# A hand-ordered queue by due time for the second network's first gemm, with copied seeds and swapped banks

## The chip, the cores and the metric

The kernel runs on one core of a Trainium2 chip. TensorE (PE in the profile) does the matmuls, VectorE (DVE), ScalarE (ACT) and GpSimd (POOL) the elementwise work, and SyncE (SP) issues nearly all DMAs. The metric is the device time of one execution in microseconds; the figure for the kernel is the median of its timed runs.

## The reference

Attention in chunks of 64 rows, then two feed-forward networks, each with a wide hidden layer, all in fp32:

```python
x = attn_out.transpose(0, 2, 1, 3).reshape(4608, 512)
h = x @ w1_in                     # 512 -> 2048
x = leaky_relu(h, 0.01) @ w1_out  # 2048 -> 512
h = x @ w2_in                     # 512 -> 2048
P = a[0] + a[1]*h + a[2]*h*h + a[3]*h*h*h
Q = 1 + abs(b[0])*abs(h) + abs(b[1])*h*h
out = (P / (Q + 1e-6)) @ w2_out   # 2048 -> 512
```

## The kernel before

The 4608 rows are cut into nine blocks of 512 columns (the data lie transposed). PE works in a format that keeps only part of an fp32 mantissa, so every operand is split into a high part (an ACT copy into that format) and a low part (a DVE subtract), and each product is three matmul passes: high by high, high by low, low by high (`PASSES`, L417). One matmul is 128x128 by 128x512.

The first part (start-up and the loop at L1134) runs attention and the first network block by block: `gemm1` (L550) is 12 matmuls, `gemm2` (L582) 12 matmuls, two of the eight PSUM banks (`hh_ps`) hold the first gemm's results in turn, four (`o_acc`) the second's. Beside it the second network's weights are decoded and staged to DRAM (`stage_w`, L414). The finished blocks go to DRAM as `xd`, through four `ypool` buffers. One step of 24 matmuls makes one of 16 hidden slices `f` of a block.

`second` (L733) does the rest. Its first loop (L889) makes block 8's first network, its second (L927) block 0's second network. Between the two parts `hh_ps` grows from two banks to four (L1181).

Then come 32 *units* (L1019), eight for each of four pairs of blocks. A unit makes two hidden slices of both blocks of the pair by a Strassen-like form: seven `product`s (L972, 6 matmuls each) take the place of eight, of ready-made sums of the weights (`wa`, S1 to S4) and of the blocks (`T1` to `T4`, made by POOL in `sums_make`, L748), and of plain parts (A11, A12, A22 with `B11`, `B21`, `B22`). The results lie in four banks a, b, c, d. In the order of the queue: `a = A11·B11`, ACT copies a to SBUF (L1043), `b = A12·B21`, DVE adds the copy onto b (L1048); `a += S2·T2`, ACT copies a (L1055); `a += S3·T3`, ACT copies a (L1062); `c = S1·T1`, DVE forms `d = c + copy` (L1067); `a += A22·T4`; `c += S4·B22`, and DVE adds the second copy onto c (L1091). Between the products stand three or four *tasks* (`task`, L825): the 12 matmuls of the second gemm for one earlier hidden slice.

The rational function of a bank pair is ten kinds of steps. `begin` (L982) runs on ACT: two times `Abs` (L992), the linear part of Q over both (L993), two times the linear part of P (L863). `act_q` (L866) is on POOL; `act_p1`, `act_p2` (L869, L872) on DVE read the bank; `act_l` is a reciprocal root and a square on ACT (L875, L876); `act_r`, `act_g` (L879, L882, L883) are three 128x1024 DVE instructions. `pre`/`split` (L821, L808) then make the high part (ACT, L813) and the low part (DVE, L814) for the next task just ahead of it. At a change of pair the new blocks' forms are loaded (`x_load`) and split (`x_split`, L769: a 128x1024 ACT copy and a 128x1024 DVE subtract), and where a block's 16 tasks end, `finish` (L617) empties the four `o_acc` banks. After the units 20 tasks remain.

Every engine works off its own queue in the order of the program text (`manual_schedule`): there is no planner in this part, the order is that of the lines L1019 to L1115.

Of the kernel before, what the change touches and what calls it, by code (L numbers as in the profile page):

```python
# [9 lines left out]
F32 = mybir.dt.float32  # L10
# [33 lines left out]
NPAIRS = 4  # L44

# [169 lines left out]
def tile_kernel(ctx: ExitStack, tc: tile.TileContext, qt, kt, vt, w1, w2, a, b, out):  # L215
# [40 lines left out]
    xf = [dram.tile([4, P, 2, TM], F32, name=f"xf{j}") for j in range(NPAIRS)]  # L256

# [312 lines left out]
    def act1b(i, f):  # L570
        t = gt[0, i, f]
        gh, gl = (gpool.tile([P, TM], F32R, tag=g, name=f"{g}0_{i}_{f}")[:, :BLOCKS[i]] for g in ("gh", "gl"))
        nc.scalar.activation(out=gh, in_=t, func=AF.Copy)  # L573
        gt[0, i, f] = gh, gl, t
# [42 lines left out]
    def finish(ph, i, share=False, cut=False):  # L617
        n = BLOCKS[i]
        for dc in range(KC):
            y = ypool.tile([P, TM], F32, tag="y", name=f"y{ph}_{i}_{dc}")[:, :n]  # L620
            dst = out[dc, :, starts[i]:starts[i] + n] if ph else xd[i][dc]
            for c, r in enumerate([slice(0, n // 2), slice(n // 2, n)] if cut and dc == KC - 1 else [slice(0, n)]):
# [4 lines left out]
                nc.sync.dma_start(out=dst[:, r], in_=y[:, r])  # L627

# [99 lines left out]
    FORMS = ("B11", "B21", "T2", "T3", "T1", "T4", "B22")  # L728
# [4 lines left out]
    def second(npool):  # L733
# [14 lines left out]
        def sums_make(j, q, t, eng):  # L748
            kc, c = q // 2, slice(q % 2 * 256, q % 2 * 256 + 256)
            for x, a, b, op in ((3, 3, 1, "subtract"), (1, 1, 0, "subtract"), (0, 3, 0, "add"), (2, 2, 0, "subtract")):  # L750
                eng.tensor_tensor(out=t[:, x], in0=t[:, a], in1=t[:, b], op=getattr(ALU, op))
            for x, nm in ((1, "T1"), (0, "T2"), (3, "T3"), (2, "T4")):
                nc.sync.dma_start(out=xf[j][SUMS[nm]][:, kc, c], in_=t[:, x])
# [3 lines left out]
        def x_load(j, n):  # L757
# [3 lines left out]
            i0, i1 = blocks_of(j)  # L761
            if nm in SUMS:
                src = xf[j][SUMS[nm]]
            else:
                i, k = {"B11": (i0, 0), "B21": (i0, 2), "B22": (i1, 2)}[nm]
                src = xd[i][k:k + 2].rearrange("k p n -> p k n")
            nc.sync.dma_start(out=t[:, 1].bitcast(F32), in_=src)

        def x_split(j, n):  # L769
            t = xform[j, FORMS[n]]  # L770
            S.activation(out=t[:, 0], in_=t[:, 1].bitcast(F32), func=AF.Copy)
            V.tensor_tensor(out=t[:, 1], in0=t[:, 1].bitcast(F32), in1=t[:, 0].bitcast(F32), op=ALU.subtract)
# [18 lines left out]
        def load_o(q):  # L791
            t = wo[q] = wpool.tile([P, 2, 2, DM], F32R, tag=TAGO[q % 3], name=f"wo{q}")
            for x in range(2):
                nc.sync.dma_start(out=t[:, x].bitcast(F32), in_=wd[2 * (q % HALF) + x][:, :, 1, :])

# [6 lines left out]
        for j in range(NPAIRS):  # L802
            for i in blocks_of(j):
                tasks.extend((1, i, f) for f in range(NF))
        halved, done = [0], [0]
        free, left_of = [], {}
# [426 lines left out]
```

## Time and profile before

| | us |
|---|---|
| median of the timed runs (lowest, highest) | 1741.75 (1740.11, 1743.24) |
| the profiled execution | 1752.58 |
| its span, first to last instruction | 1750.7 |
| mean granted share of the TensorE clock | 0.975 |

The profile is one execution. Busy time of an engine is the time in which one of its instructions ran; matmuls overlap in the pipeline, so a matmul's listed duration is longer than its share of PE's time. The clock of PE is listed as a share of the full one (2.4 GHz); 0.5 is the lower of its two levels (1.2 GHz).

### The profile page before, as it was taken

To read this page: it belongs to the slowest core of one execution; us is meant where nothing else is said; L and a number is where in the kernel's file an instruction comes from. 1 tells how busy PE (TensorE), PEld (TensorE's weight loads), DVE (VectorE), ACT (ScalarE), POOL (GpSimd) and SP (SyncE) were. 2 spreads that over 40 slices of the span, in tenths; PEclk is the share of its full clock that TensorE was granted. 3 is DMA by queue.
4 is the path that set the end of the run, shared out by engine and by line. 5 is a ranking of instruction groups with operands and counts; after the bars stand their busy time and mean duration, and the time that the engine had idled before them with its cause. 6 is when DMAs were issued, how large, how long until landed. Compare 5 with 4: busy or idle time off the path is not lost.

```text
span 1750.7 us, 24111 instructions
## 1 busy us (share of the span) xinstructions
PE 1653.1 (94%) x9198; PEld 1340.8 (77%) x9198; DVE 1210.7 (69%) x1825; ACT 926.6 (53%) x1418; POOL 260.4 (15%) x157
## 2 busy tenths in 40 slices
PE   8999999999999999999999988899989998899989
PEld 7888788888888888888777776677767776677767
DVE  8984766565656665632875787877878787877772
ACT  7653233333333333334766676666667666666652
POOL 0000000000000000000222341243213332122110
PEclk9999999999999999999999998999989999999999
DMA  7631324343343343326645675567556675556425
GB/s 273 221 109 43 101 92 139 103 133 119 111 144 115 119 129 124 100 94 207 210 139 177 203 260 181 183 211 238 204 175 223 216 262 192 167 179 196 141 89 182
DMA packets 143571, 284.71 MB, mean 163 GB/s; under 512 B 12384, under 2 KB 45408, under 8 KB 138208
## 3 DMA queue, kind: packets, MB, share of 16 engines
q1 hardware_dynamic: 143024, 282.51, 48.5%
q8 instruction: 73, 1.20, 0.3%
q10 hardware_dynamic: 432, 0.66, 0.1%
q14 instruction: 42, 0.34, 0.1%
HBM read 229.64 MB, written 53.48 MB: 162 GB/s over the span
## 4 chain that ended last, share of the span: by engine, by line
PE 67%; ACT 18%; DVE 10%; issue 3%; DMA 1%; POOL 0%; SPq 0%; ACTq 0%; DVEq 0%; POOLq 0%
PE hh L558 23%; PE hh L975 11%; PE oa L591 10%; PE ob L591 10%; PE oa L836 5%; PE ob L836 4%; ACT u L993 3%; DVE gl L814 3%; ACT ah L992 3%; ACT l L876 2%; ACT sa L863 2%; ACT l L875 2%; ACT gh L813 2%; ACT sb L863 1%; PE at L458 1%
## 5 line engine op out<-in xcount | busy, mean ns | idle before, releaser
L558 PE MATMUL hh<-x,w 128*128 128x512 f32 x1920 | 459.9, 390 | 0.1
L558 PEld LDWEIGHTS hh<-x,w 128*128 128x128 f32 x1920 | 359.7, 188 | 75.4 <-DVE x L543 0.5
L866 POOL TENSOR_TENSOR u<-u,ah 128x1024 f32<-128x1024 f32 x64 | 163.8, 2559 | 559.2 <-ACT u L993 556.4
L567 ACT ACTIVATE t<-hh 128x512 f32<-128x512 f32 x128 | 76.5, 597 | 315.2 <-PE hh L558 301.5
L836 PE MATMUL oa<-gh,wo 128*128 128x512 f32 x576 | 215.6, 414 | 15.1 <-DVE y L624 7.6
L975 PE MATMUL hh<-xf_T,wa 128*128 128x512 f32 x576 | 162.9, 432 | 62.5 <-ACT s L1043 62.4
L836 PE MATMUL ob<-gh,wo 128*128 128x512 f32 x576 | 202.2, 392 | 0.0
L975 PEld LDWEIGHTS hh<-xf_T,wa 128*128 128x128 f32 x576 | 115.3, 205 | 99.1 <-ACT s L1043 75.6
L578 DVE TENSOR_TENSOR gl<-t,gh 128x512 fp32r<-128x512 f32 x128 | 88.3, 690 | 144.0 <-ACT gh L573 140.0
L591 PE MATMUL oa<-gh,w 128*128 128x512 f32 x512 | 182.0, 396 | 0.0
L591 PE MATMUL ob<-gh,w 128*128 128x512 f32 x512 | 178.4, 389 | 0.0
L836 PEld LDWEIGHTS oa<-gh,wo 128*128 128x128 f32 x576 | 117.6, 204 | 44.9 <-DVE y L624 10.2
L992 ACT ACTIVATE ah<-hh 128x512 f32<-128x512 f32 x128 | 69.5, 596 | 126.7 <-DVE hh L1091 86.5
L486 POOL TENSOR_TENSOR e<-e,sm 128x512 f32<-128x512 f32 x23 | 24.0, 1044 | 710.4 <-DVE sm L482 710.4
L836 PEld LDWEIGHTS ob<-gh,wo 128*128 128x128 f32 x576 | 109.6, 190 | 23.7
L836 PE MATMUL oa<-gl,wo 128*128 128x512 f32 x288 | 120.0, 417 | 6.4 <-DVE gl L814 6.4
L836 PE MATMUL ob<-gl,wo 128*128 128x512 f32 x288 | 112.6, 391 | 0.0
L591 PEld LDWEIGHTS oa<-gh,w 128*128 128x128 f32 x512 | 96.1, 188 | 21.2
L591 PEld LDWEIGHTS ob<-gh,w 128*128 128x128 f32 x512 | 96.1, 188 | 20.2
L591 PE MATMUL oa<-gl,w 128*128 128x512 f32 x256 | 99.9, 390 | 0.0
L494 DVE STREAM_TRANSPOSE pt<-e 32x256 f32<-32x256 f32 x224 | 97.5, 435 | 3.2
L591 PE MATMUL ob<-gl,w 128*128 128x512 f32 x256 | 99.6, 389 | 0.0
(172 smaller groups left out, 2794.3 us busy)
## 6 DMA issues: line engine op xcount, KB each, us to landing
wo<-wd SPq DMA_DIRECT2D x144, 512.0 KB, 5.3
wa<-ws SPq DMA_DIRECT2D x32, 1024.0 KB, 5.1
raw<-in_w SPq DMA_DIRECT2D x46, 512.0 KB, 4.8
wb<-wd SPq DMA_DIRECT2D x32, 512.0 KB, 4.3
q<-in_q SPq DMA_DIRECT2D x36, 256.0 KB, 3.6
raw<-in_w SPq DMA_DIRECT2D x9, 1024.0 KB, 5.0
v<-in_v SPq DMA_DIRECT2D x36, 256.0 KB, 4.1
k<-in_k SPq DMA_DIRECT2D x34, 256.0 KB, 4.0
```

Of the source, the lines that this page charges most:

```text
L494: nc.vector.transpose(pt[c + b:c + b + 32, :, a:a + 32], e[c + a:c + a + 32, :, b:b + 32])
L558: nc.tensor.matmul(ps, w[wp][:, 0, kc * P:(kc + 1) * P], x[:, xp, kc, :], start=(kc == 0 and (wp, xp) == (0, 0)), stop=(kc == KC - 1 and ( ...
L567: nc.scalar.activation(out=t, in_=ps, func=AF.Prelu, alpha=0.01)
L578: nc.vector.tensor_tensor(out=gl, in0=t, in1=gh.bitcast(F32), op=ALU.subtract)
L591: nc.tensor.matmul(o_acc(dc, n), w[wp][:, 1, dc * P:(dc + 1) * P], g[gp], start=(first and (wp, gp) == (0, 0)), stop=(last and (wp, gp) == ...
L814: V.tensor_tensor(out=gl, in0=g, in1=gh.bitcast(F32), op=ALU.subtract)
L836: nc.tensor.matmul(o_acc(dc, TM), w[:, wp, c] if ph else wt[0, f][wp][:, 1, c], g[gp], start=(f == 0 and (wp, gp) == (0, 0)), stop=(f == N ...
L863: S.activation(out=t, in_=h, func=AF.Identity, scale=nega[:, 3:4], bias=nega[:, 2:3])
L866: G.tensor_tensor(out=u, in0=u, in1=ah, op=ALU.mult)
L975: nc.tensor.matmul(bank, wform[:, wp, kc * P:kc * P + P], x[:, xp, kc, :], start=start and kc == 0 and (wp, xp) == PASSES[0], stop=stop an ...
L992: S.activation(out=ah[:, x], in_=h[x], func=AF.Abs)
L993: S.activation(out=uu, in_=ah, func=AF.Identity, scale=absb[:, 1:2], bias=absb[:, 0:1])
```

## The change

What it does, in the order of the program:

- While blocks 2 to 7 run, finished blocks are read back from `xd`, split on ACT and DVE, and their high and low parts are stored in a new DRAM array `xs` (18 pieces of 128x512; six more are done in the units). The forms B11, B21, B22 are then loaded split, 1 MB each instead of 512 KB, and need no `x_split`.
- `hh_ps` stays at two banks (d and c in the units); the other two become one tile `hab` of two banks, a and b. From unit to unit a and b change places.
- In a unit the copies go into banks as starting values: ACT copies a into b (PE then accumulates A12·B21 onto it) and a into c (PE accumulates S1·T1 and S4·B22). S3·T3 goes into d alone, is copied to SBUF by ACT, and DVE adds it onto a and forms `d = c + copy`. So DVE has two adds instead of three.
- The steps on the pair (a, b) read both banks with one 128x1024 instruction; those on (c, d) stay 128x512.
- High and low parts are made for two hidden slices at a time (`split_hi`, `split_lo`, 128x1024), further ahead of the task than before.
- Each step of the units and of the tasks behind them is put in a list with a due time (`at`), unit `u` at `20.43*u` plus an offset; the list is sorted and issued in that order.
- Five units have three tasks (before: four units), so 21 tasks remain after the units instead of 20. Block 8's second gemm accumulates in the banks of a to d, and the last two tasks of block 7 stand behind the first four of block 8.

```diff
+UNIT = 20.43
+            if ph == 0 and 0 < i < NB - 2 and (i % 2 or dc > 1):
+                later.append((i, dc))
+    def split_out(i, dc, y):
+        half = xs[(i - 1) // 2][dc // 2 if i % 2 else 2]
+        hi, lo = (ypool.tile([P, TM], F32R, tag="y", name=f"y{c}{i}_{dc}") for c in "hl")
+        nc.scalar.activation(out=hi, in_=y, func=AF.Copy)
+        nc.vector.tensor_tensor(out=lo, in0=y, in1=hi.bitcast(F32), op=ALU.subtract)
+        for c, z in enumerate((hi, lo)):
+            nc.sync.dma_start(out=half[:, c, dc % 2, :], in_=z.bitcast(F32))
+    def reload(i, dc):
+        y = ypool.tile([P, TM], F32, tag="y", name=f"yr{i}_{dc}")
+        nc.sync.dma_start(out=y, in_=xd[i][dc])
+        return y
...
+        FEWER = {0: 0, 1: 1, 2: 3, 4: 1, 5: 3}
+        SLOTS = (1.36, 5.45, 13.62, 17.7)
+        order = [(u, x) for u in range(NU2) for x in range(4) if x != FEWER.get(u)] + [(NU2, x) for x in range(NF + 8)]
...
+        def split_hi(p):
+            t0, t1 = tasks[2 * p:2 * p + 2]
+            g, sub, first = twos.pop(t0)
...
+            S.activation(out=gh, in_=g, func=AF.Copy)
+        def split_lo(p):
...
+            gl = gpool.tile([P, 2, TM], F32R, tag="g", name=f"gl_{p}")
+            V.tensor_tensor(out=gl, in0=g, in1=gh.bitcast(F32), op=ALU.subtract)
...
+        for p in range(HALF + 1, len(tasks) // 2):
+            u, x = when[2 * p]
+            if u < NU2:
+                hi, lo = ((-UNIT + 8.35, -UNIT + 14.3), (-UNIT + 10.2, 1.4), (-UNIT + 10.2, 1.4), (8.35, 14.3))[x]
...
         for u in range(NU2):
             j, k = divmod(u, HALF)
+            a, b = ab[:, u % 2], ab[:, 1 - u % 2]
+            mm(0.0, "A11", "B11", a, True)
+            mm(4.09, "S2", "T2", a, False)
+            mm(1.36 if FEWER.get(u) == 0 else 8.17, "S3", "T3", d, True)
+            mm(9.53, "A22", "T4", a, False)
+            mm(10.9, "A12", "B21", b, False)
+            mm(12.26, "S1", "T1", c, False)
+            mm(16.34, "S4", "B22", c, False)
...
+            at(u, 1.45, copy, b, a)
+            at(u, 5.5, copy, c, a)
+            at(u, 9.6, keep)
+            at(u, 12.3, add, a, a)
+            at(u, 13.6, add, d, c)
+            at(u, 13.0, lin, u, 0)
+            at(u, 14.2, mag, u, 0)
+            at(u, 15.2, lin, u, 1, 1)
+            at(u, 16.0, den, u, 0)
+            at(u, 17.2, mag, u, 1, 1)
+            at(u, 17.9, lin, u, 1, 0)
+            at(u, 18.7, mag, u, 1, 0)
+            at(u, 19.3, den, u, 1)
+            at(u, UNIT + 2.2, root, u, 0)
+            at(u, UNIT + 3.5, square, u, 0)
+            at(u, UNIT + 6.1, root, u, 1)
+            at(u, UNIT + 7.2, square, u, 1)
+            at(u, 17.4, den_q, u, 0)
+            at(u, 20.6, den_q, u, 1)
+            at(u, 15.6, cube, u, 0, 0)
+            at(u, 16.8, cube, u, 0, 1)
+            at(u, 18.1, cube, u, 1, 0, 1)
+            at(u, 18.8, cube, u, 1, 1, 1)
+            at(u, 19.5, cube, u, 1, 0, 0)
+            at(u, 20.2, cube, u, 1, 1, 0)
+            at(u, UNIT + 4.4, rest, u, 0)
+            at(u, UNIT + 8.4, rest, u, 1)
...
+                        at(u, 12.35 + 1.05 * x, sums, k - 2, x)
...
+                    at(u, 2.65, x_lo, j + 1, 1)
+                    for x, t in enumerate((1.42, 5.48, 9.58, 10.95, 12.28)):
+                        at(u, t, x_load, j + 1, 2 + x)
+                    at(u, 11.3, x_hi, j + 1, 2)
+                    at(u, 12.4, x_hi, j + 1, 3)
+                    at(u, 12.35, x_lo, j + 1, 2, G)
+                    at(u, 14.0, x_lo, j + 1, 3, G)
+                    at(u, UNIT + 0.7, x_hi, j + 1, 5)
+                    at(u, UNIT + 2.65, x_lo, j + 1, 5)
+        for _, _, fn, args in sorted(events):
+            fn(*args)
...
+                split_later()
                 if f != 1:
                     stage_w()
                 if f in (3, 6, 9, 11, 13):
                     stage_w()
+                if f > 1:
+                    reload_later()
...
-        hh_ps.extend(singles(ps_open("hhq", "right"), "hh2", "hh3"))
+        at_new = ps_open("hhq", "right").tile([P, 2, TM], F32, name="hab")
```

In the new names `lin`, `mag`, `den`, `den_q`, `root`, `square`, `cube` and `rest` are the steps L863, L992, L993, L866, L875, L876, L869 with L872, and L879 with L882 and L883; `add` is a DVE add, `keep` and `copy` are ACT copies, `mm` is a `product`. `G` is POOL.

## Rows read from the trace of the kernel before

**Rows 1.** The page's first parts: span, and the granted clock by slices.

```profile
span 1750.7 us, 24111 instructions
...

```

**Rows 2.** The cores' view: span and mean granted clock.

```profile
core 0: 1750.7 us, clock 0.975
```

**Rows 3.** Stretches: length, busy PE, PEld, DVE, ACT, POOL (instructions), clock, DMA share, GB/s.

```profile
40.00:826.00 786.00, 785.98 (x5221) 645.42 (x5220) 489.71 (x938) 304.31 (x514) 25.31 (x24) 1.00 0.37 122
...
910.00:1747.00 837.00, 749.73 (x3074) 599.85 (x3072) 623.31 (x735) 533.01 (x737) 216.17 (x113) 0.95 0.58 193
...
913.00:1684.00 771.00, 692.69 (x2836) 554.74 (x2837) 595.40 (x699) 508.46 (x701) 212.54 (x111) 0.95 0.59 197
```

**Rows 4.** PE's waits, 910 us to the end: us in total, times, longest.

```profile
PE hh L975 <- ACT s L1043: 62.4, 27, 4.2
PE oa L836 <- DVE y L624: 7.6, 6, 1.7
PE oa L836 <- DVE gl L814: 6.4, 8, 1.3
PE oa L836 <- ACT gh L813: 4.2, 1, 4.2
PE oa L836 <- ACT y L626: 3.2, 1, 3.2
PE hh L975 <- DVE sa L872: 2.7, 1, 2.7
```

**Rows 5.** The chain that ended last, through one unit: start, us, what.

```profile
1393.74 0.62 DVE hh L1091
...
1394.44 1.09 ACT ah L992 x2
...
1400.79 0.49 ACT s L1043
...
1401.32 1.66 PE hh L975 x6
```

**Rows 6.** PE's timeline later in that unit: start, us, line, count.

```profile
1405.54 2.88 PE L975 MATMUL hh<-xf_T,wa 128*128 128x512 f32 x12
1408.26 1.52 PE L975 MATMUL hh<-xf_T,wb 128*128 128x512 f32 x6
```

**Rows 7.** Stretches, PE alone, behind waits of 1.71 and 2.97 us.

```profile
1417.00:1424.00 7.00, 5.29 (x24) 1.00 0.98 362
...
1444.00:1452.00 8.00, 5.03 (x17) 0.80 0.07 26
```

**Rows 8.** Single lines on DVE and POOL: ns least/median/most, first and last start.

```profile
L879 DVE SCALAR_TENSOR_TENSOR u<-u,l x64: 1215/1218/1768, 943.0 to 1696.0; 128x1024 f32<-128x1024 f32 x64
...
L772 DVE TENSOR_TENSOR xf_B<-xf_B x12: 1215/1218/1219, 839.9 to 1511.9; 128x1024 fp32r<-128x1024 f32 x12
...
L1048 DVE TENSOR_TENSOR hh<-hh,s x32: 683/691/700, 920.6 to 1667.7; 128x512 f32<-128x512 f32 x32
...
L866 POOL TENSOR_TENSOR u<-u,ah x64: 2359/2405/3414, 931.1 to 1686.3; 128x1024 f32<-128x1024 f32 x64
```

**Rows 9.** The timeline where POOL and DVE overlap: start, us, engine, line.

```profile
1119.57 2.79 POOL L866 TENSOR_TENSOR u<-u,ah 128x1024 f32<-128x1024 f32 x1 [15.53 <-ACT u L993]
1120.03 2.87 DVE L814 TENSOR_TENSOR gl<-sa,gh 128x512 fp32r<-128x512 f32 x1
```

**Rows 10.** Groups in the units: shapes, count, busy us, mean ns, idle before.

```profile
L993 ACT ACTIVATE u<-ah,absb 128x1024 f32<-128x1024 f32 x63 | 78.4, 1244 | 2.1
L875 ACT ACTIVATE l<-u,cst 128x1024 f32<-128x1024 f32 x62 | 70.8, 1142 | 0.0
...
L1043 ACT ACTIVATE s<-hh 128x512 f32<-128x512 f32 x32 | 18.5, 578 | 2.5 <-PE hh L975 2.5
...
L883 DVE SCALAR_TENSOR_TENSOR gn<-gn,nega,u 128x1024 f32<-128x1024 f32 x17 | 21.8, 1285 | 0.6
```

More of the change, by code (lines that the diff above doesn't have):

```diff
@@ L731, in tile_kernel, with second @@
     NU2 = NPAIRS * HALF
-    def second(npool):
+    def second(npool, at_new):
         S, G = nc.scalar, nc.gpsimd
@@ L898, in second @@
             if 4 <= f < 8:
-                sums_make(0, f - 4, st[f - 4], V)
+                for x in range(4):
+                    sums_make(0, f - 4, st[f - 4], V, x)
             if 2 <= f < 6:
@@ L970, in second, with product @@
         live = {}
-        def product(wform, x, bank, start, stop):
+        ab, (d, c) = at_new, hh_ps[:2]
+        def product(wform, x, bank, start):
             for kc in range(2):
@@ new lines, in den_q, with root, square, cube @@
+        def den_q(u, r):
+            act_q(*live[u, r][1:3])
+        def root(u, r):
+            v = live[u, r]
+            S.activation(out=v[1], in_=v[2], func=AF.Abs_reciprocal_sqrt, bias=cst[:, 0:1])
+        def square(u, r):
+            v = live[u, r]
+            S.activation(out=v[1], in_=v[1], func=AF.Square)
+        def cube(u, r, step, x=None):
+            t = live[u, r][0]
+            (act_p1, act_p2)[step](ab if x is None else (c, d)[x], t if x is None else t[:, x])
+        def rest(u, r):
+            v = live.pop((u, r))
+            act_r(v[2], v[1])
+            act_g(v[2], v[1], v[0])
@@ new lines, in second @@
+        for n in range(2 * HALF, len(tasks)):
+            ph, i, f = tasks[n]
+            if f == NF - 1 and n + 1 < len(tasks):
+                u, x = when[n]
+                t = SLOTS[x] if u < NU2 else 2.72 * x
+                for dc in range(KC):
+                    eng = (S, V, S, V)[dc] if x < 3 or u == NU2 else (V, V, S, S)[dc]
+                    at(u, t + 0.72 + (0.64 if u == NU2 or x < 3 else 0.9) * dc, put, i, dc, eng)
+        at(0, 1.5, finish_one, NF - 1)
+        back = {}
@@ new lines, in add @@
+            def add(to, of, u=u):
+                V.tensor_tensor(out=to, in0=of, in1=live[u, 2], op=ALU.add)
+            if u == 0:
+                at(u, 0.05, lambda b=b: nc.tensor.matmul(b, wb[0][:, 0, 0:P], xform[0, "B11"][:, 0, 0, :], start=True, stop=True))
+            at(u, 1.45, copy, b, a)
[5 more added lines that the diff above has]
+            at(u, 14.2, mag, u, 0)
```

308 lines of the change are left out of this document (152 added, 156 removed).

## Prediction, made before the changed kernel ran

> **What bounds the kernel now.** I read the page first, then the stretches, then PE's waits, then the chain through one unit.
>
> The page gives a span of 1750.7 us and shows the granted clock below full only in the last part [rows 1]. The stretches say the same: from 40 to 826 us PE is busy for 785.98 of 786.00 us at full clock, so nothing but fewer matmuls could shorten that part, and ACT and DVE have room there (304 and 490 us of 786). From 910 to 1747 us PE is busy for 749.7 of 837 us, with 3072 matmuls (1344 in products, 1728 in tasks; the row counts two more at its edges), at a clock of 0.95 [rows 3].
>
> The pace of matmuls without waits: twelve start within 1408.26 - 1405.54 = 2.72 us, 0.2267 us each [rows 6]. So 3072 matmuls need 696.4 us, and the 837 us hold some 140 us of something else. Two things make it up.
>
> Waits: 62.4 us in 27 of the 32 units for the copy L1043, and 24.1 us in 17 others, 86.5 us in all [rows 4]. A listed matmul lasts 2.88 - 11 x 0.2267 = 0.39 us [rows 6], and the next one may start after 0.23, so each vanished wait also gives back 0.16 us of pipeline end: 44 x 0.16 = 7.0 us.
>
> Clock: the mean over the run is 0.975 [rows 2], and it is 1.00 before 910 us, so 0.025 x 1750.7 = 43.8 us of full-rate time are lost behind 910 us. Part of that falls into waits; with PE busy for 749.7 of 837 us [rows 3], 0.896 x 43.8 = 39.2 us hit matmuls. The fall to the lower level (1.2 GHz) comes behind the longer waits: clock 0.80 around a wait of 2.97 us, 1.00 around one of 1.71 us [rows 7].
>
> 86.5 + 7.0 + 39.2 = 132.7 us; the remaining 8 us are short hand-overs.
>
> Why the copy is late: S2·T2 accumulates on a, so it needs L1043's copy of a. That copy is behind, on ACT, all of the previous unit's (c, d) work, which starts only when DVE has finished the add L1091: from 1393.74 (add) through ACT's queue to 1400.79 (copy) and PE at 1401.32 [rows 5]. It is a ring through DVE, ACT and PE, and PE has only 24 matmuls (5.44 us) to cover a chain of 7.6 us.
>
> **The change part by part.**
>
> *The ring is cut.* In the new queue, L1091's add is gone (c is seeded before its products), and ACT comes to the seed copy with nothing left behind: its last step of the unit before, `den` at 19.3, lasts 1.24 us [rows 10] and ends at 20.5, and A11·B11 ends at 20.43 + 1.36 + 0.16 = 21.95. I lay out one unit, times from its start. A seed copy into PSUM by ACT is not in this trace; an ACT copy out of PSUM takes 0.58 [rows 10], a DVE instruction that writes PSUM 0.69 to 0.70 [rows 8]. I take 0.58, the same engine. It ends at 2.1 (2.2 with the dearer price); S2·T2 is due at 4.09: 1.9 us to spare. Then root and square (at most 1.14 each [rows 10]) to 4.4, the second seed 5.6 to 6.2 for S1·T1 at 12.26. The other links: `add` on a needs A22·T4 (10.9) and `keep`, the add into d needs S1·T1, so 13.8 to 14.5, and S4·B22 on c, due at 16.34, has 1.8 us to spare. DVE's `split_lo` follows, 1.22 [rows 8], to 15.7, for the task at 17.7: 2 us to spare. Then two `cube` steps on (a, b); a 128x1024 instruction from PSUM is not shown; between 1.22 to 1.29 (128x1024 from SBUF [rows 8, 10]) and 1.40 (twice the 0.70 of a 128x512 one with a PSUM operand [rows 8]) I take 1.29, as the fixed part is paid once. They end at 18.3 and free the bank of the next A11·B11 at 20.43: 2.1 us to spare, 1.9 by the dearer price. No product stands behind a chain without at least 1.8 us of cover.
>
> *Load of the engines.* ACT: 508.5 us in 32 units = 15.9 each [rows 3]; nothing but the two PSUM destinations gets dearer, up to 2 x 0.12, and of seven `x_split` copies per pair four stay: under 16.2 of 20.43. DVE: 595.4 / 32 = 18.6 [rows 3]; one add less (0.69), and five of seven `x_split` subtracts per pair less (two stay on DVE, two go to POOL, three end): 5 x 1.22 / 8 = 0.76. So 17.15. Against this stands the lock between POOL and DVE. A DVE instruction with both sources in SBUF that starts while POOL runs lasts until POOL is done and then its own time: 2.87 us in place of 0.69 beside a POOL instruction [rows 9]; one with a PSUM operand keeps its 0.69 to 0.70 throughout [rows 8]. The new `split_lo` due at 1.4 meets `den_q` of the unit before (due 0.17, 2.4 us [rows 8], to 2.6): 1.2 us of waiting. The one due at 14.3 meets pieces of `sums` in half the units, up to 1.05 by their due times: 0.5 on average. 17.15 + 1.2 + 0.5 = 18.9 us of 20.43, 1.5 to spare. The first wait ends the subtract at 3.8, before the task at 5.45 and `rest` at 4.4.
>
> *The other waits.* L624 and L626 (10.8 us): where a block's tasks end, the next task used to stand right behind; now at least a product or more lies between (next slot 4.09 us later, four copies at about 0.6 on two engines). L814 and L813 (10.6): high and low parts are made at least 1.6 us ahead, as laid out. L872 (2.7): unit 0 begins with products in banks of its own; but its S3·T3 uses d, one of the only two banks that the loop of block 0 now has, so I leave 1.2 us there. At the three changes of pair two subtracts stand on POOL in front of `den_q` and may hold DVE's `split_lo` past 17.7: 0.5 us each. Behind unit 31 `rest` and a `split_lo` share DVE ahead of the fourth task: 1.3 us. Left over: 4 us.
>
> *What is added elsewhere.* 18 pieces in blocks 3 to 7: an ACT copy (0.58), a DVE subtract (0.69) and three 256 KB DMAs each, in steps of 5.44 us, 24 matmuls. ACT would rise from 39% to 40% and DVE from 62% to 64% there [rows 3]; a step's first-gemm bank is needed again only two steps later, which hides a few us of delay. I cost it at nothing; with that cover gone it would be 18 x 1.3 = 23 us. The DMA share of the units, 0.59 over 771 us [rows 3], becomes about 0.59 x 24.1 / 20.43 = 0.70. On SP the loads of the next pair's forms stand behind a weight load that waits for its task: the one due at 1.42 leaves at 4.1, and its copy is due at 11.3. With two banks in place of four, block 8's loop still gives ACT 2.72 us from the end of one gemm to the next use of its bank. Nothing here.
>
> **The sum**, on the profiled execution: 1750.7 - 132.7 + 4 = 1622.0 span, with 1.9 us around it 1623.9. The median is 1741.75 against 1752.58 for that execution, 0.9938 of it: 1614 us. The floor is 910 + 696.4 + 4 (behind the last matmul) = 1610 span, 1602 in the median's terms.
>
> **The rivals.**
>
> *The clock goes on falling* although the long waits go. For it: PE would still have short hand-overs. Against it: the row of a 1.71 us wait at full clock [rows 7]. It gives back 39 us: 1653. On this the Trainium skill, "TensorE: Matmul & The Clock Gate", section "A second HAM failure mode: psum-queue depth-cycling", tells of a kernel in which short but frequent idling between groups of matmuls made the clock swing between its levels. By that rule this rival; by the trace, the forecast.
>
> *DVE becomes the bound.* 18.9 of 20.43 leaves 1.5. If one `den_q` falls into `rest`, whose sources are all in SBUF, DVE needs 18.9 + 2.4 = 21.3, and each unit 0.9 us more: 32 x 0.9 = 29, so 1643.
>
> *The wait only changes its place*, so the change does not do what it says: another link (a seed, the add into d) holds PE about as long per unit, 62 us of wait and the clock with it. Only the 24 us of other waits go: about 1717. Against it: every link has 1.8 us to spare in the layout.
>
> *Slower.* The queues are fixed by due times. If ACT's `den` on (c, d) comes 1.8 us late, its `den_q` ends at 4.4 instead of 2.6 and runs into `rest`; DVE falls behind, everything slides, and both `den_q` and all `sums` end up against instructions with SBUF sources. DVE then needs 18.9 + 4.8 + 1.6 = 25.3 us a unit, 4.9 over PE's: 32 x 4.9 = 157, so 1771. It decides against the change from 4.0 us a unit on (128 us in all). For it: the lock is in the rows [rows 9]. Against it: `den` would have to be late on an engine with 4 us of room per unit.
>
> **How the numbers follow.** Forecast 0.60 (own range 1602 to 1632), DVE bound 0.15 (to 1658), clock 0.12 (1653), wait elsewhere 0.07, slower 0.06. The likeliest is the forecast, 1614. The range from the floor, 1602, to 1658 holds the first three, 0.87; a narrower one would cut into the clock's case. Faster by over 0.2% (about what a measurement of this kernel can tell) are all but the last: 0.93; 0.01 for the same; 0.06 slower.
>
> **What would show it.** Right: a stretch from 910 us to the end about 133 us shorter, PE's waits under 10 us in total, clock 1.00 behind 910 us, 20.4 us a unit. DVE bound: PE waits for DVE lines, DVE busy over 95% in the units, low parts of 3 us and more. The clock: waits gone, mean clock still 0.975. Wrong altogether: units of 24 us, or PE idle between 215 and 826 us, where the 18 pieces run.

## The result, and the profile after

The changed kernel takes 1623.76 us (median of four executions, 1622.95 to 1624.04). The kernel before takes 1742.49 beside it (median of four, 1740.11 to 1753.17). The ratio is 0.9307 with an interval of 0.9268 to 0.9345: 6.9% faster, 119 us less. The forecast was 1614 in a range of 1602 to 1658. The span came out at 1620.7 where the sum said 1622.0.

The page of the kernel after: span, busy times with their share and count, PE's busy tenths in 40 slices, and the granted clock in the same slices.

```profile
span 1620.7 us, 24054 instructions
...
PE 1603.5 (99%) x9199; PEld 1317.1 (81%) x9199; DVE 1211.5 (75%) x1665; ACT 908.8 (56%) x1292; POOL 264.3 (16%) x163
...
PE   8999999999999999999999999999999999999998
...
PEclk9999999999999999999999999999999999999999
```

PE is busy from end to end, and the clock never shows a fall. Before, two slices of the same line are below nine tenths, both in the last part, and the mean was 0.975 [rows 2]:

```profile
PEclk9999999999999999999999998999989999999999
```

Stretches of the kernel after, columns as in [rows 3]: the first part, all behind 910 us, the units, and three units in which POOL makes no sums.

```profile
40.00:826.00 786.00, 784.87 (x5215) 644.59 (x5215) 504.30 (x954) 313.43 (x531) 25.97 (x24) 1.00 0.43 140
...
910.00:1617.00 707.00, 701.32 (x3082) 577.00 (x3080) 612.78 (x561) 508.06 (x596) 218.53 (x119) 1.00 0.71 242
913.00:1567.00 654.00, 649.05 (x2854) 534.36 (x2852) 594.87 (x545) 497.39 (x583) 217.79 (x119) 1.00 0.73 248
1434.84:1496.04 61.20, 61.20 (x272) 50.68 (x270) 54.72 (x49) 44.44 (x52) 14.42 (x6) 1.00 0.58 194
```

The stretch behind 910 us was 837 us with 749.73 of them busy on PE [rows 3]. It is 707 us now, with about as many matmuls. 3082 of them at 0.2267 us each [rows 6] need 698.7, so 8.3 us are left of the 140 that were lost. The last row is three units in which PE is busy for all of 61.20 us: 20.40 a unit, 90 matmuls at that pace. The first part is as long as it was, with DVE and ACT a little fuller.

PE's waits from 910 us to the end: us in total, times, longest, as in [rows 4].

```profile
PE hh L903 <- DVE gl L887: 1.3, 1, 1.3
PE hab L1063 <- DVE gn L953: 1.2, 1, 1.2
PE hab L1063 <- DVE sb L953: 1.1, 1, 1.1
PE hab L903 <- ACT yl L935: 0.7, 1, 0.7
PE hab L1063 <- ACT hab L1176: 0.7, 1, 0.7
PE oa L903 <- DVE gl L887: 0.6, 1, 0.6
```

Six waits of 5.6 us in place of 44 of 86.5 us. None repeats from unit to unit.

The start of one unit at 1312.44, where the two events lie that the layout was worked out for: the seed copy and the lock between POOL and DVE. Columns: start, us, engine, line, operation, count, idle time before and its releaser.

```profile
1312.44 1.52 PE L1063 MATMUL hab<-xf_B,wb 128*128 128x512 f32 x6
...
1312.54 2.39 POOL L947 TENSOR_TENSOR u<-u,ah 128x1024 f32<-128x1024 f32 x1 [0.85 <-ACT u L1102]
1312.79 3.23 DVE L887 TENSOR_TENSOR gl<-sb,gh 128x1024 fp32r<-128x1024 f32 x1
...
1314.00 0.58 ACT L1176 ACTIVATE hab<-hab 128x512 f32<-128x512 f32 x1 [1.53 <-PE hab L1063]
...
1316.52 0.84 PE L1063 MATMUL hab<-xf_T,wa 128*128 128x512 f32 x3
```

The counts of the last row end with the view, at 1317. ACT stood idle for 1.53 us, waiting for the product A11·B11, so in this unit nothing was queued ahead of the copy any more. The copy ends at 1314.58, and S2·T2, which may write a from then on, starts at 1316.52: 1.94 us of cover where [rows 5] had a wait. The low part (L887) started under `den_q` (POOL L947) and ended 3.58 us into the unit.

Single lines of the kernel after: ns least/median/most, first and last start.

```profile
L1176 ACT ACTIVATE hab<-hab x32: 573/582/601, 915.0 to 1538.4; 128x512 f32<-128x512 f32 x32
L1176 ACT ACTIVATE p<-hh x32: 576/600/600, 918.8 to 1547.0; 128x512 f32<-128x512 f32 x32
...
L887 DVE TENSOR_TENSOR gl<-sb,gh x22: 1217/3028/3233, 1020.0 to 1600.9; 128x1024 fp32r<-128x1024 f32 x22
```

A copy into PSUM lasts 0.582 us, one from PSUM to SBUF 0.600. The 22 low parts made from the `sb` tiles take 1.22 us at least and 3.03 in the median; the 46 made from `sa` and `gn`, the same line, have medians of 1.33 and 1.24.

### The profile page after: what moved, and what is told of

Same layout as the page of the kernel before. It is cut to its first block, busy times and chain, and to the rows that moved or that the text cites. A ratio compares the mean times of both kernels' runs of the same rounds, so it can differ in the third digit from the quotient of the medians.

```text
span 1620.7 us, 24054 instructions
## 1 busy us (share of the span) xinstructions
PE 1603.5 (99%) x9199; PEld 1317.1 (81%) x9199; DVE 1211.5 (75%) x1665; ACT 908.8 (56%) x1292; POOL 264.3 (16%) x163
## 4 chain that ended last, share of the span: by engine, by line
PE 87%; DVE 6%; ACT 4%; issue 1%; DMA 1%; SPq 0%; ACTq 0%; DVEq 0%
PE hh L560 24%; PE oa L594 11%; PE ob L594 10%; PE ob L903 10%; PE oa L903 10%; PE hab L1063 10%; PE hh L1063 7%; PE hab L903 1%; PE hh L903 1%; PE at L460 1%; PE at L532 1%; ACT us L941 1%; DVE us L963 1%; DVE us L960 1%; DVE u L960 1%
## 5 line engine op out<-in xcount | busy, mean ns | idle before, releaser
L947 POOL TENSOR_TENSOR u<-u,ah 128x1024 f32<-128x1024 f32 x64 | 154.3, 2413 | 275.1 <-ACT u L1102 262.0
L594 PE MATMUL oa<-g,w 128*128 128x512 f32 x768 | 198.8, 394 | 0.0
L594 PE MATMUL ob<-g,w 128*128 128x512 f32 x768 | 194.8, 389 | 0.0
L581 DVE TENSOR_TENSOR g<-t,g 128x512 fp32r<-128x512 f32 x128 | 90.5, 707 | 123.9 <-ACT g L576 119.5
L594 PEld LDWEIGHTS ob<-g,w 128*128 128x128 f32 x768 | 144.2, 188 | 30.2
L594 PEld LDWEIGHTS oa<-g,w 128*128 128x128 f32 x768 | 141.9, 188 | 30.2
L903 PEld LDWEIGHTS oa<-gh,wo 128*128 128x128 f32 x512 | 96.1, 188 | 20.4 <-DVE y L923 0.5
L1063 PE MATMUL hab<-xf_B,wb 128*128 128x512 f32 x384 | 97.7, 390 | 2.3 <-DVE gn L953 1.2
L496 DVE STREAM_TRANSPOSE pt<-e 32x256 f32<-32x256 f32 x224 | 97.5, 435 | 3.2
L1063 PE MATMUL hh<-xf_T,wa 128*128 128x512 f32 x384 | 97.4, 389 | 0.0
L960 DVE SCALAR_TENSOR_TENSOR u<-u,ah 128x1024 f32<-128x1024 f32 x64 | 78.2, 1222 | 23.5 <-ACT ah L1113 23.4
L1063 PEld LDWEIGHTS hab<-xf_B,wb 128*128 128x128 f32 x384 | 71.8, 188 | 18.3 <-DVE sb L953 1.7
L576 ACT ACTIVATE g<-t 128x512 fp32r<-128x512 f32 x128 | 80.6, 630 | 6.7 <-PE ob L594 3.8
```

What stands on the lines that cost most here:

```text
L496: nc.vector.transpose(pt[c + b:c + b + 32, :, a:a + 32], e[c + a:c + a + 32, :, b:b + 32])
L581: nc.vector.tensor_tensor(out=gl, in0=t, in1=gh.bitcast(F32), op=ALU.subtract)
L594: nc.tensor.matmul(o_acc(dc, n), w[wp][:, 1, dc * P:(dc + 1) * P], g[gp], start=(first and (wp, gp) == (0, 0)), stop=(last and (wp, gp) == ...
L903: nc.tensor.matmul(acc(ph, i, dc), w[:, wp, c] if ph else wt[0, f][wp][:, 1, c], g[gp], start=(f == 0 and (wp, gp) == (0, 0)), stop=(f == ...
L947: G.tensor_tensor(out=u, in0=u, in1=ah, op=ALU.mult)
L960: V.scalar_tensor_tensor(out=u, in0=u, scalar=C1, in1=l, op0=ALU.add, op1=ALU.mult)
```

## Why the error was in the last step: executions of the kernel before

The sum gave 1623.9 us for the device time and the kernel takes 1623.76. The forecast of 1614 came from the last step, which scaled by 0.9938 because the profiled execution of the kernel before was longer than the median. The first run asks what that surplus was. It is the kernel before, unchanged.

> The kernel before, unchanged, to see the clock and span of each of its runs. Theory A (its runs differ because the waits of about 2 us let the clock fall in some units and not in others, so the profiled execution was simply one with more falls): the runs' spans differ by up to 13 us, and their mean clocks with them, about 0.975 at a span of 1751 and 0.981 or more at 1738 (each 0.001 of clock is 1.75 us of full-rate time). Theory B (the profile itself costs 0.6%, as the prediction's last step took it): unprofiled runs have the same clock, 0.975, and a span about 10 us shorter.

Measured: 1743.58 us (median of ten, 1740.30 to 1753.29), a ratio of 0.9992 (0.9961 to 1.0023) to its own runs beside it. Each execution's time with its granted clock, the profiled one first:

```
1745.00 0.980   1741.93 0.982   1753.29 0.975   1741.35 0.983   1751.66 0.975
1741.64 0.983   1742.16 0.983   1740.30 0.983   1753.23 0.975   1751.17 0.975
```

The times fall into two groups, and the clock divides them: 1751 to 1753 us at 0.975, 1740 to 1745 at 0.980 to 0.983. So the surplus of the execution in [rows 2] was not a constant share that belongs to profiling. It was clock falls, and the sum had already taken those away with the 39.2 us. The changed kernel, at clock 1.00, has none, and its executions agree within 1.1 us.

The waits themselves are the same in the profiled executions of both groups: 62.4 us in 27 for the copy L1043 at clock 0.975, 62.6 in 26 at 0.980. What differs is which of them the clock falls behind. Two stretches that begin with the same wait of 3.3 us for that copy, the first in the execution of [rows 2], the second in this run, the columns of [rows 3]:

```profile
1050.83:1060.12 9.29, 6.00 (x16) 4.75 (x16) 8.61 (x11) 6.43 (x9) 1.23 (x1) 0.63 0.26 88
```

```profile
1050.76:1060.04 9.28, 6.00 (x26) 4.99 (x27) 8.60 (x11) 6.53 (x10) 1.22 (x1) 1.00 0.24 84
```

So the falls come behind longer waits, but not behind each. Over the 8 us from its start, a wait of 1.97 us for that copy shows 0.79 in ten of 13 cases in [rows 2]'s execution and 1.00 in three.

## Experiments on what the gain is made of

**One step exchanged in the kernel before.** The ring in the prediction says that S2·T2 waits because work of the unit before is queued ahead of the copy L1043 on ACT. Here one such step, the reciprocal root and the square (L875, L876) of one bank pair, is moved behind the copy. Nothing else changes.

```diff
-            on(v, 0, "l")
             on(v, 1, "p1")
...
             S.activation(out=sw[:, 0], in_=a, func=AF.Copy)
+            on(v, 0, "l")
```

> The kernel before with one step moved in ACT's queue: the root and square of the previous unit's (a, b) pair stand behind the copy L1043 instead of ahead of it. Theory A (the waits were a chain that was 2 us too long, mostly by what stood ahead of the copy on ACT): the copy comes 2.2 us sooner, the 62.4 us of waits for it fall to 10 to 20, most of the clock's falls go, and the time is 1660 to 1690. Theory B (only seeds, wider look-ahead and due times cut the ring, and a mere exchange moves the wait to the next link): 1725 to 1745, with waits of some 2 us a unit for another line.

Measured: 1706.92 us (1705.57 to 1708.33), ratio 0.9753 (0.9722 to 0.9785). The cores' view, and PE's waits from 910 us on (the copy is L1042 here):

```profile
core 0: 1704.2 us, clock 0.988
...
PE hh L975 <- ACT s L1042: 12.2, 15, 2.0
PE hh L975 <- DVE xf_B L772: 9.4, 3, 3.1
PE oa L836 <- DVE gl L814: 7.1, 10, 2.3
PE oa L836 <- DVE y L624: 6.3, 3, 2.2
PE hh L975 <- ACT s L1055: 5.9, 15, 1.3
```

The wait for the copy fell from 62.4 us to 12.2, as the theory of ACT's queue has it. The time fell by 36 us against 1742.49 (the runs of before beside this one had more executions at the lower clock, a median of 1750.85, hence the ratio), more than a mere change of place would give and less than the theory gave. It lies in neither theory's band. The rest is in other links: the loaded forms' split (L772), the second copy (L1055), the low parts; all of PE's waits behind 910 us are 53.4 us where they were 86.5, and the clock is 0.988. The order on ACT alone is worth 30 to 36% of the gain (36 of 119 us, or by the ratios 2.5 of 6.9%); the remaining links have to be given slack too.

**The change with the copy late again.** If the gain is waits and clock, putting the wait back must cost just that. In every unit but the first, ACT gets five, then eight copies of a ahead of the seed copy, each 0.58 us, with 1.94 us of cover.

```diff
+        def more_act(u, a):
+            for _ in range(5):
+                S.activation(out=live[u - 1, 2], in_=a, func=AF.Copy)
...
+            if u:
+                at(u, 1.44, more_act, u, a)
             at(u, 1.45, copy, b, a)
```

> The changed kernel with five more ACT copies of bank a (0.6 us each, into a tile that nobody needs then) ahead of the seed copy in each unit but the first, so that the seed comes 3.0 us later and S2·T2, which had 1.9 us of cover, waits about 1.1 us in each unit. Theory A (waits this short do not bring the clock down): 31 x 1.1 = 34 us more, 1645 to 1670, clock 1.00. The rival on the clock (short, frequent idling makes it fall): 20 to 40 us on top, with a mean clock under 0.99.

> The same with eight more copies: the seed comes 4.8 us later and S2·T2 waits about 2.9 us in each unit. Theory A (waits of this length bring the clock down, as in the kernel before, where a fall cost some 1.7 us): 31 x 2.9 = 90 us of waits and 31 to 53 us of clock, 1740 to 1770, mean clock about 0.97. If the clock had nothing to do with waits: 90 us alone, 1714, clock 1.00.

Measured: 1679.82 us (1679.17 to 1683.05), ratio 0.9637 (0.9605 to 0.9670) with five; 1768.58 (1767.28 to 1772.39), ratio 1.0140 (1.0100 to 1.0180) with eight. PE's waits from 910 us on and the stretch from 910 us, first with five copies (L1180 is the seed copy):

```profile
PE hab L1063 <- ACT hab L1180: 37.2, 32, 2.0
PE oa L903 <- DVE gl L887: 5.6, 4, 3.3
PE hh L1063 <- DVE hh L1187: 3.8, 4, 1.5
...
910.00:1674.00 764.00, 715.33 (x3080) 576.13 (x3078) 619.86 (x561) 591.58 (x750) 232.80 (x119) 1.00 0.66 224
```

and with eight:

```profile
PE hab L1063 <- ACT hab L1180: 93.3, 32, 3.6
PE hh L1063 <- DVE hh L1187: 4.3, 6, 1.9
PE oa L903 <- DVE gl L887: 4.1, 5, 3.2
...
910.00:1767.00 857.00, 750.51 (x3081) 601.06 (x3079) 630.02 (x562) 650.37 (x844) 241.91 (x119) 0.95 0.59 200
```

32 waits of 1.16 us on average, at most 2.0, leave the clock at 1.00 in that stretch (0.998 over the run). 32 waits of 2.92 us on average bring it to 0.95 (0.975 over the run), the level of the kernel before; the commonest, of 2.87 us, is followed by a fall in 12 of 22 cases. So the rival that short idling keeps the clock falling is refuted for waits of about 1 us, one to a unit, and the prediction's reading, that the longer waits bring it down, holds. The Trainium skill ("TensorE: Matmul & The Clock Gate", section "A second HAM failure mode: psum-queue depth-cycling") tells of a kernel in which frequent short idling between groups of matmuls made the clock swing. With one wait to a unit, these rows show that for waits near 3 us and not for those near 1 us; shorter and more frequent idling is in no run here.

The run with five copies is 10 us above its expected band, since the delayed copy makes other links late: L887 and L1187 hold 9.4 us. The run with eight lets the prediction's arithmetic be tried backwards. Waits for the copy 93.3, the pipeline ends 32 x 0.16 = 5.1, L1187 4.3, L887 4.1 - 0.6 = 3.5, and the clock: 0.025 x 1770.2 = 44.3 us, of which 750.5 / 857 = 0.876 hit matmuls, 38.8. The sum is 145.0. The rows come from an execution with a span of 1770.2 us, 149.5 more than the 1620.7 of the changed kernel's: 97% of it is found. (That 1623.8 + 145.0 = 1768.8 meets the median of 1768.58 is partly luck, since this execution was the slowest of its four, 1772.39.)

## Experiments on the parts of the change

**The banks a and b keep their roles.**

```diff
-            first = 1 - u % 2 if r == 0 else 0
+            first = 1 if r == 0 else 0
...
-            a, b = ab[:, u % 2], ab[:, 1 - u % 2]
+            a, b = ab[:, 0], ab[:, 1]
```

> The changed kernel with a and b in fixed banks instead of changing places each unit. Theory A (both banks are read to the end by the same 128x1024 instructions, so the next A11·B11 waits for the same thing in either bank): 1621 to 1627, the same as changed. Theory B (the exchange frees a bank earlier): PE waits for cube steps in each unit, 0.5 us or more each, 1640 or more.

Measured: 1623.44 us (1622.53 to 1623.48), ratio 0.9275 (0.9239 to 0.9310, to the same runs of before as the exchanged step's). The exchange of the banks is worth nothing that can be measured here; the units are 20.40 us long either way.

**B11, B21 and B22 loaded whole and split in the units.** The 18 pieces of the first part and the six of the units end, and the `x_split` steps stand in the units again.

```diff
-                later.append((i, dc))
+                pass
...
-        XSTEP = {3: 1, 4: 2, 5: 3, 7: 5}
+        XSTEP = {s: s - 2 for s in range(2, 9)}
...
+                if k == 5:
+                    at(u, 11.3, x_hi, j + 1, 0)
...
+                    at(u, UNIT + 8.36, x_hi, j + 1, 6)
+                    at(u, UNIT + 12.1, x_lo, j + 1, 6)
```

> The changed kernel without operands stored split: B11, B21 and B22 are loaded whole and split in the units by ACT and DVE again, and the 18 pieces beside the first part and the six in the units are gone. Theory A (the splits fit into the room that ACT and DVE have; three more subtracts of 1.22 us a pair cost PE at most a few us at the three changes of pair, and what the first part loses now, about 1 us, comes back): 1622 to 1632. Theory B (the stored split carries a good part of the gain, since the units at a change of pair were the longest before, 28 to 31 us): 1640 or more, with those units above 23 us.

Measured: 1624.38 us (1623.23 to 1625.72), ratio 0.9316 (0.9287 to 0.9345). The first part of this kernel:

```profile
40.00:826.00 786.00, 785.98 (x5222) 645.62 (x5221) 489.83 (x938) 305.37 (x517) 24.76 (x24) 1.00 0.37 122
```

PE's idle time in the first part is 0.02 us here against 786.00 - 784.87 = 1.13 in the kernel after, which has one wait of 1.1 us there (in attention, L532 for DVE's L496). So the 18 pieces cost about 1.1 us, where the prediction took nothing and held 23 as the other end. The other runs whose first part is that of the changed kernel have the same wait, 0.8 to 1.4 us. What the pieces spare the units is as little: with the splits back, the units at a change of pair take 20.4 to 21.5 us, and the time is the same within its spread.

**The last bank without a seed.** S3·T3 accumulates on a again, its copies go to SBUF, c begins with S1·T1, and DVE adds a copy onto c behind S4·B22, as it did before.

```diff
-            mm(1.36 if FEWER.get(u) == 0 else 8.17, "S3", "T3", d, True)
-            mm(9.53, "A22", "T4", a, False)
-            mm(10.9, "A12", "B21", b, False)
-            mm(12.26, "S1", "T1", c, False)
+            mm(8.17, "S3", "T3", a, False)
+            mm(9.53, "A12", "B21", b, False)
+            mm(10.9, "A22", "T4", a, False)
+            mm(12.26, "S1", "T1", c, True)
...
+            at(u, 5.5, keep, 3)
+            at(u, 9.6, keep, 2)
+            at(u, 13.6, add, d, c, 2)
+            at(u, 17.85, add, c, c, 3)
```

> The changed kernel without the seed in c: the copy of a goes to SBUF, S3·T3 accumulates on a as before, c starts with S1·T1, and DVE adds the copy onto c behind S4·B22, the add that stood in the old ring. As many DVE adds as in the changed kernel. Theory A (the order and the distance of the steps carry the gain; with 1.9 us of cover the longer chain through c still fits): 1624 to 1640, clock 1.00. Theory B (the seed in c is what cut the ring): waits of 2 us or more return in most units and the clock falls, 1690 or more.

Measured: 1658.10 us (1657.15 to 1658.91), ratio 0.9474 (0.9444 to 0.9505), so neither theory's band. The largest wait of PE from 910 us on (L1176 is ACT's copies), and the timeline where it falls in one unit:

```profile
PE hab L1063 <- ACT k L1176: 23.4, 34, 0.7
...
1302.78 1.52 PE L1063 MATMUL hab<-xf_B,wb 128*128 128x512 f32 x6
...
1304.34 0.60 ACT L1176 ACTIVATE k<-hab 128x512 f32<-128x512 f32 x1 [1.76 <-PE hab L1063]
...
1304.99 1.20 PE L1063 MATMUL hab<-xf_T,wb 128*128 128x512 f32 x4 [0.69 <-ACT k L1176]
```

The copy reads a, which was complete when A12·B21 began at 1302.78. Yet it starts only when that product, which writes b, has ended, and A22·T4 then waits for the copy. a and b are the halves of one tile, `hab`. A further run puts the copy ahead of A12·B21 in the queue.

```diff
-            at(u, 9.6, keep, 2)
+            at(u, 9.52, keep, 2)
```

> As the kernel without the seed in c, but with the copy of a after S3·T3 queued ahead of A12·B21 and not behind it. There ACT waited for the end of A12·B21, which writes the other half of the pair tile, and PE then waited 0.7 us in each unit, 23.4 us in all. Theory A (the seed in c is not what the gain needs): these waits go, 23.4 us and 34 x 0.16 of pipeline end, so 1658 falls to 1629 or less, 1622 to 1632. Theory B (the longer chain through c costs of itself): 1640 or more, with waits for other lines.

Measured: 1667.59 us (1666.32 to 1668.75), ratio 0.9559 (0.9533 to 0.9585). The same place in a unit:

```profile
PE hab L1063 <- ACT k L1176: 30.7, 34, 2.2
...
1329.36 0.60 ACT L1176 ACTIVATE k<-hab 128x512 f32<-128x512 f32 x1 [0.40 <-PE hab L1063]
...
1330.01 1.20 PE L1063 MATMUL hab<-xf_B,wb 128*128 128x512 f32 x4 [0.69 <-ACT k L1176]
```

Now the product into b waits for the copy that reads a. In either order the tile of two banks is waited for as a whole: 0.69 us and a pipeline end of 0.16 per unit, (0.69 + 0.16) x 32 = 27 us of the 34 that the first of the two costs; in the second some of these waits are longer, and 30.7 + 34 x 0.16 = 36 of its 44 us are found. So it went by neither theory: the waits did not go, and they are for the same line. The kernel after meets it once a unit, on DVE, where a is complete before A12·B21 begins (1302.92) and the add onto a starts only at its end:

```profile
1302.92 1.52 PE L1063 MATMUL hab<-xf_B,wb 128*128 128x512 f32 x6
...
1304.55 0.70 DVE L1183 TENSOR_TENSOR hab<-hab,p 128x512 f32<-128x512 f32 x1 [0.23 <-PE hab L1063]
```

No matmul into a stands behind that add in the unit, so nothing waits. S3·T3 in d, a tile of its own, keeps the copies clear of it. In the kernel before, where a to d are four tiles, the like copy overlaps: L1062 copies a behind S3·T3, while the second six of the twelve matmuls that begin at 1405.54 and end at 1408.42 [rows 6], S1·T1, write c.

```profile
1407.10 0.60 ACT L1062 ACTIVATE s<-hh 128x512 f32<-128x512 f32 x1 [2.69 <-PE hh L975]
```

So two banks as such do not keep a copy and a matmul apart; these rows say that what is waited for is the tile.

What c's own chain (copy, product, add on DVE) costs is small. From unit 8 on a unit of the first kernel takes 21.38 us, 0.98 more than 20.40. 0.85 of it is the wait for the pair tile, which leaves 0.13 us a unit, and PE waits for no add onto c. ACT still comes early to the seed copy: in the unit at 1314.64 it ends at 1316.78, 1.94 us ahead of S2·T2. So in this layout the add that stood in the old ring does not bring the ring back, and the seed in c is not what cuts it. What is left is the order and the distance of the steps, of which the exchanged step above is one. No run takes out by themselves the seed in b, the two-bank steps or the earlier high and low parts; what each is worth stays open.

## Experiments on DVE's room

DVE is busy in 594.87 of 654 us in the units, 18.6 us of 20.40, and 54.72 / 3 = 18.2 in the units without sums. The rival said that it becomes the bound. Two runs give it two or four more 128x512 subtracts a unit, on a tile that is no longer used; a third gives POOL two more.

```diff
+        def more_dve(u):
+            for _ in range(2):
+                V.tensor_tensor(out=live[u - 1, 2], in0=live[u - 1, 2], in1=live[u - 1, 2], op=ALU.subtract)
...
+            if u:
+                at(u, 3.0, more_dve, u)
```

The second has `range(4)`. The third issues the two on POOL, due at 4.5, beside `rest`.

> The changed kernel with two more 128x512 subtracts on DVE in each unit but the first, 1.4 us, ahead of the first rest, on a tile that nobody needs then. Theory A (DVE needs about 18.6 us of the 20.4 of a unit, so 1.4 us still fit, for the most part in its idle time ahead of rest): at most 10 us more, up to 1634, clock 1.00. Theory B (DVE's order already sets the units, and any addition is paid in full): 31 x 1.4 = 43 us more, 1667.

> The same with four more subtracts, 2.8 us a unit. Theory A: 18.6 + 2.8 = 21.4 us of DVE against 20.4 of PE, so about 1.0 us a unit more, 31 us, 1645 to 1665, and PE's waits stay near 1 us each, so the clock stays at 1.00. The rival on the clock (short, frequent waits make it fall): 20 us or more beyond that, with a mean clock of 0.99 or less. Theory B: 86 us more, 1710.

> The changed kernel with two more 128x512 subtracts on POOL in each unit but the first, 2.6 us, due in the middle of rest, whose sources lie in SBUF; POOL is busy for a third of a unit only. Theory A (POOL and DVE exclude each other for such instructions): DVE loses up to 2.6 us a unit with not one instruction more, 18.6 + 2.6 = 21.2 of 20.4, so 15 to 35 us more, 1639 to 1659, and single instructions of rest last up to 2.5 us. Theory B (no such exclusion, POOL has room): the same as changed, 1621 to 1627.

Measured: two on DVE 1637.42 us (1633.14 to 1638.85), ratio 0.9387 (0.9355 to 0.9418); four 1690.11 (1688.66 to 1690.89), ratio 0.9692 (0.9662 to 0.9722); two on POOL 1641.97 (1639.89 to 1644.10), ratio 0.9413 (0.9377 to 0.9450). Three units without sums in each kernel, in this order, the columns of the stretches:

```profile
1450.46:1511.66 61.20, 61.20 (x271) 50.69 (x270) 58.99 (x58) 45.77 (x54) 15.82 (x7) 1.00 0.58 193
```

```profile
1495.07:1558.64 63.57, 62.32 (x271) 50.09 (x270) 61.12 (x61) 43.62 (x51) 14.24 (x7) 1.00 0.57 190
```

```profile
1455.80:1517.00 61.20, 61.20 (x272) 50.69 (x270) 59.02 (x51) 45.07 (x54) 27.15 (x13) 1.00 0.58 195
```

With two more on DVE its busy time rises by (58.99 - 54.72) / 3 = 1.42 us a unit, and PE is still busy throughout: 20.40. With four, DVE is busy in 61.12 of 63.57 us and the unit is 21.2 long: DVE is the bound there. So 2.2 us of room, in these units, is real, and the rival is refuted for the kernel as it stands. By the medians, two on DVE come out 3 us above theory A's limit of 1634, two on POOL inside theory A's band, and four 25 us above it. Two more POOL instructions raise DVE's time as much, by 1.43 us a unit, with no instruction added on DVE: that is the lock. It holds POOL up as well: its added subtracts take 1.04 us at least and 1.91 in the median. One place in that kernel's timeline:

```profile
1460.06 4.00 POOL L1126 TENSOR_TENSOR p<-p 128x512 f32<-128x512 f32 x2
...
1461.10 2.06 DVE L960 SCALAR_TENSOR_TENSOR u<-u,ah 128x1024 f32<-128x1024 f32 x1
```

L960 lasts 1.23 us without POOL beside it and 2.06 here. The 14 and 18 us that these two kernels cost lie elsewhere: among units 2 to 4 (up to 4.2 us longer than in the changed kernel), in units 9 to 14 (20.4 to 21.3 us) and at the changes of pair (21.9 to 24.5). The sums alone do not use up the room. Units 18 to 21 make sums too, DVE is busy there for 74.19 / 4 = 18.5 us a unit in the changed kernel, and with either addition they stay at 20.40. In units 10 to 13 it is 75.81 / 4 = 19.0, since three of the six pieces are split there; the room is about 1.4 us, and neither addition fits in whole: these four units come to 20.8 to 20.9 us on average.

With four subtracts units 10 to 13 and 18 to 21 become 21.6 to 23.8 and those at a change of pair 26 to 27, and the clock falls to 0.99, 0.01 x 1687 = 17 us of the 66. That is the time and the clock which the expectation gave to the clock's rival, but the falls are not behind short waits. The longest waits behind 910 us of that kernel (L1187 is the add into d, or onto a):

```profile
PE hh L1063 <- DVE hh L1187: 32.2, 22, 4.0
```

Behind four of the 22, those of 3.58 to 4.02 us, the clock falls (0.64 to 0.82 over the wait and the next 6 us); behind the other 18, of 0.32 to 2.38 us, it stays at 1.00.

## An attempt at the waits that are left

The loop of block 0, from 826 to 910 us, starts 356 matmuls in 84.00 us in the changed kernel. At 0.2267 us each they need 80.7, so 3.3 us are lost there, and the first units and the epilogue lose a few more. This version moves the splits in that loop one step ahead, and makes two low parts behind the units earlier.

```diff
-            pre(2)
+            pre(3)
...
+            if u == NU2 and x in (3, 5):
+                hi, lo = {3: (1.0, 2.3), 5: (6.5, 8.3)}[x]
```

> The changed kernel with two places mended where PE still waits: in block 0's loop the low part of a task is made one task earlier (pre(3) in place of pre(2)), and behind the last unit two split_lo stand ahead of the two rests. The first costs PE now 0.35 us in each of some 13 steps (5.79 in place of 5.44 us), the second 1.3 us. If nothing else slips: 1.3 + 0.16 + 13 x 0.35 = 6 us less, 1617 to 1619. If DVE's and ACT's own ring bounds that loop's steps, the first brings nothing: 1622.

Measured: 1623.23 us (median of six, 1622.59 to 1625.19), ratio 0.9307 (0.9284 to 0.9330): no gain that can be told from none. The loop's stretch and the largest wait behind it:

```profile
826.00:910.00 84.00, 84.00 (x371) 69.30 (x370) 62.98 (x90) 58.66 (x92) 19.28 (x15) 1.00 0.58 201
...
PE hab L1063 <- ACT hab L1178: 3.5, 1, 3.5
```

PE is busy for the whole loop now (371 matmuls), and the loss comes back as one wait of 3.5 us for the first unit's seed copy. The unit begins at 908.51 and not at 911.88, but the copy starts at 914.52, where it was 914.99. ACT and DVE were hardly done any earlier; their own work in the loop sets when the first unit's copy can run. No version faster than the changed kernel was found.

## Why the prediction was right, and where it was wrong

*The bound and the ring.* Right, and shown by the runs that put the wait back. The stretch behind 910 us is 130 us shorter (133 forecast), PE's waits there are 5.6 us (under 10), the clock 1.00, a unit 20.40 us. From the rows of after, the gain splits as the prediction split it: waits 86.5 - 5.6 = 80.9, pipeline ends 38 x 0.16 = 6.1, clock 39.2, together 126 of the 130 us of span; the rest is short hand-overs, of which the prediction expected some 8 to stay and 2 did. That the seed in c cuts the ring, as the prediction also had it, is not borne out: without it PE waits for the pair tile and not for the add onto c. The longer waits do bring the clock down, but the two rows of 2.97 and 1.71 us [rows 7] are no border: the same wait shows a fall in one case and none in another.

*The last step.* Wrong, and nearly the whole error. Scaling by 0.9938 took the surplus of one execution for a constant share, though the same argument had named its source, the clock, and removed it. Unscaled the forecast was 1623.9. The price that should have stood there is the distance from span to device time alone, 1.9 us by the rows of before, 2.2 now. That the unscaled sum then meets the median within 0.2 us is partly luck. It stands for the profiled execution, which took 1622.95, and its terms miss both ways: the hand-overs that stay are 6 us smaller, waits and pipeline ends 5.6 + 6 x 0.16 = 6.6 us where 4 was left, and the first part loses 1.1 us where nothing was counted.

*The seeds.* Right. 0.58 us taken for an ACT copy into PSUM, 0.582 measured; 1.9 us of cover ahead of S2·T2, 1.94 measured; the add into d due at 13.8 to 14.5, and in the unit at 1312.44 it starts 13.80 us in. What the layout did not see is that a and b are waited for as one tile: DVE's add onto a stands behind A12·B21, which writes b, and the slack there covers it.

*The two-bank steps.* 1.29 us taken for a `cube` step of 128x1024, 1.21 and 1.28 measured for the two.

*Load of the engines.* ACT under 16.2 us a unit, 497.39 / 32 = 15.5 measured. DVE 18.9 with the lock, 18.6 measured. The low part under `den_q` ends at 3.6 us where 3.8 was worked out; it starts at 0.35 and not at 1.4, so it is held for 2.0 us and not 1.2. The 0.5 us for the sums was reckoned for half the units, but sums are made in 12 of 32, and the six pieces split in the units, 0.69 us of DVE each, were left out. That the lock costs DVE time in that way was argued from one pair of rows [rows 9]; the run with more work on POOL shows it, 1.43 us a unit. The mean of 18.9 hid that the room is not even: 2.2 us in the units without sums, 1.9 in units 18 to 21 with them, and about 1.4 in units 10 to 13 with sums and pieces.

*The rivals.* DVE as the bound: wrong by 2.2 us of room, but two subtracts more would have cost 14 us, four 66. One of the signs named for it, low parts of 3 us and more, did appear, with DVE busy for 91% and not over 95%. The clock: refuted for waits near 1 us, one to a unit. The wait elsewhere: no link repeats in PE's waits. The slower case needs 4 us a unit; nothing here came near it, except by adding 4.6 us of ACT work ahead of one copy.

*Costed at nothing.* The 18 pieces cost 1.1 us. The DMA share of the units is 0.73 where 0.70 was estimated, and no transfer is among the waits behind 910 us.

*Left over.* 4 us assumed, 5.6 of waits found: two of 1.1 and 1.2 us for the `cube` step (L953) on the next unit's banks, between 940 and 1040 us, among the first six units, of which five have three tasks and so are 2.7 us shorter; the prediction laid out only a unit with four. One of 1.3 lies behind unit 31, as named, and one of 0.7 at 915 us for the first seed copy. The 0.5 us at each change of pair did not show.

## What to carry to other kernels

When a wait in a repeating unit is caused by one engine's queue, ask what stands ahead of the instruction waited for, and move that work behind it. A copy that PE accumulates onto can take the place of an add on a third engine; here it works, but the kernel without the seed in c has no wait for that add either. Cost the granted clock as a term of its own, beside the waits that bring it down, and then don't also scale for a profiled execution that was longer than the median: the surplus and the clock are the same microseconds. Lay out the room per kind of unit and not as a mean, and give two banks that are read and written in turn by different engines a tile each unless one instruction really takes both: here one tile for two banks cost 0.85 us a unit as soon as a copy and a matmul met in it.

## What the runs showed of the hardware that was not expected

The kernel before has executions at two levels of the granted clock, 0.975 and about 0.982, and they are 10 us apart; with the waits gone the changed kernel's agree within 1.1 us. 32 waits of 1.16 us on average leave the clock full and 32 of 2.92 us take 0.025 of it over the run. Between them the length does not decide: behind 13 waits of 1.97 us the clock fell ten times, behind 22 of 2.87 us twelve times. Copies by ACT into PSUM are no dearer than into SBUF (0.582 and 0.600 us). A copy from one bank of a two-bank tile and a matmul into the other bank did not overlap in either order, 0.69 us a unit, while the copy L1062 of the kernel before overlaps the matmuls into another bank that is a tile of its own. That points to the program's bookkeeping by tiles and not to the banks.
